# Folding w3 with w_out by plain f32 products, w_out converted in place, instead of by three products of high and low parts

## The chip, the cores and the metric

The kernel runs on one core of a Trainium2 chip. The metric is the device time of one execution in microseconds. TensorE is called PE, VectorE DVE, ScalarE ACT, GpSimd POOL, and SyncE, whose queue issues almost all loads, SP. What separates two versions from no change is about 0.3% (2.5 us).

## What is computed

Windowed attention (4 sequences of 576 tokens, 8 heads of 64) gives 2304 tokens of 512 values; two linear stages follow.

```python
x = attention(q, k, v)                     # 2304 x 512
a, b = x @ w1, x @ w2                      # 512 x 1024 each
y = (a * b) @ w3 @ w_out                   # w3 1024 x 1024, w_out 1024 x 512
h = y @ w_in                               # 512 x 2048
out = maximum(0.01 * h, h) @ w_out2        # 2048 x 512
```

The weights arrive as 64-bit words and are turned into f32 on the chip.

## The kernel before, in words

Since nothing nonlinear stands between w3 and w_out, the kernel first forms wf = w3 @ w_out ("the fold") and then uses (a*b) @ wf. Nearly all large products are made of three: each f32 operand is split into a high part, rounded to the type float32r, and the low part that is left, and `mm3` (L75 to L77) issues high x high, high x low and low x high.

A weight is converted in **units** of 512 KB (128 x 512 words). A unit is loaded (L280, four buffers `raw`), scaled on ACT (`f`, L299), its low bits fetched on ACT (`low`, L287, one buffer), shifted and merged on DVE (L316), given its sign on DVE (L311), and then finished. L311 is the last reader of the raw buffer: the load four units later waits for it. SP issues loads in one fixed order, with the loads of q, k and v for the first sequence between them: none behind the first six units, one behind each of the next ten, six behind each of the next eight.

Units 0 to 15 alternate between w3 (first half of its rows) and w_out, units 16 to 23 are the second half of w3, and from unit 24 on come w1 and w2. A w3 unit is finished by four transposes on PE (L353), the copy of the high part on ACT (L355) and the low part on DVE (L356). A w_out unit is finished by a cast on ACT (L260) and a subtraction on DVE (L261). Then the fold runs in sixteen **steps**, 0 to 7 for the first half of wf and 8 to 15 for the second. Step i multiplies the i-th transposed tile, which is unit 2i up to step 7 and unit i + 8 after it, with a tile of w_out, into four banks of 512 columns: 12 matmuls. After steps 7 and 15 the four banks are copied out as wf (L372 on ACT, L373 on DVE).

Attention of the first sequence is woven between the steps, twelve groups of scores (L176 on PE, plain f32), exponentials (L184), transposes (L203, copied by L205 to `pts`) and products with v (L230, copied by L236 to `x`). When the fold is done, the products x @ w1 and x @ w2 begin (tile `ab` at L75 to L77). A scheduler fixes each engine's order when the kernel is built, and each engine then runs its list strictly in that order.

Of the kernel before, what the change touches and what calls it, by code (L numbers as in the profile page):

```python
# [8 lines left out]
F32 = mybir.dt.float32  # L9
F32R = mybir.dt.float32r  # L10
# [4 lines left out]
ALU = mybir.AluOpType  # L15
# [6 lines left out]
def tile_kernel(ctx: ExitStack, tc: tile.TileContext, q, k, v, w1, w2, w3, w_out, w_in, w_out2, out):  # L22
# [18 lines left out]
    P = 128  # L41
# [4 lines left out]
    KF = DFF // P  # L46
# [10 lines left out]
    UC = 512  # L57
# [7 lines left out]
    act, dve, pool, pe, sp = nc.scalar, nc.vector, nc.gpsimd, nc.tensor, nc.sync  # L65

    def f32(ap):
        return ap.bitcast(F32)
# [5 lines left out]
    def mm3(ps, lh, ll, rh, rl, first, last, more=False):  # L74
        pe.matmul(ps, lhsT=lh, rhs=rh, start=first, stop=False, skip_group_check=more)  # L75
        pe.matmul(ps, lhsT=lh, rhs=rl, start=False, stop=False, skip_group_check=more)  # L76
        return pe.matmul(ps, lhsT=ll, rhs=rh, start=False, stop=last, skip_group_check=more).ins  # L77

    const = ctx.enter_context(tc.tile_pool(name="const", bufs=1))
    wpool = tc.alloc_tile_pool(name="wpool", bufs=1)  # L80
# [7 lines left out]
    stage = tc.alloc_tile_pool(name="stage", bufs=2, side="right")  # L88
# [6 lines left out]
    p0 = tc.alloc_tile_pool(name="p0", bufs=4, reuse_waits="tile")  # L95
# [144 lines left out]
    def wslot(key):  # L240
        pl, tag, bufs = wpool, "w", 8
        if key[0] == "wo2":
            pl, tag, bufs = (po1, "w1", 4) if key[1] < 4 else (po2, "w2", 4)
        elif key[0] == "wf":
            tag, bufs = "wf", 4
        return pl.tile([P, 2, 2 * UC], F32R, name=tag, tag=tag, bufs=bufs)

    def rows2(t):
        return t.rearrange("p s (l m) -> p s l m", l=2)
# [4 lines left out]
    def store(key, half):  # L254

        def fin(f):
            if key not in slots:
                slots[key] = wslot(key)
            t, sl = slots[key], slice(UC * half, UC * half + UC)
            act.copy(t[:, 0, sl], f)  # L260
            (pool if key[0] in ("w1", "w2") else dve).tensor_tensor(out=t[:, 1, sl], in0=f, in1=f32(t[:, 0, sl]),  # L261
                                                                     op=ALU.subtract)
        return fin

    units = []
    last = {}
    slots = {}
# [14 lines left out]
    def flat(t):  # L282
        return t.rearrange("p k m -> p (k m)") if len(t.shape) == 3 else t

    def low_bits(u):
        u["low"] = stage.tile([P, UC], I32, name="low", tag="low", bufs=1)
        act.activation(out=u["low"], in_=flat(u["raw"]).bitcast(U8).rearrange("p (m e) -> p m e", e=8)[:, :, 3],  # L287
                       func=AF.Copy, scale=1.0 / 32, bias=-31.0 / 64)

    def advance(stop):  # L290

        now = dict(n_of)
        if now["scale"] < min(stop, now["load"]):
            u = units[now["scale"]]
            w = flat(u["raw"]).bitcast(I32).rearrange("p (m two) -> p m two", two=2)
            u["lo"], u["hi"] = w[:, :, 0], w[:, :, 1]
            u["f"] = stage.tile([P, UC], F32, name="f", tag="f", bufs=4)
            with tc.issue_after(pss["copy"]) if now["scale"] >= PHASE_B else nullcontext():
                act.mul(u["f"], u["hi"].bitcast(F32), 2.0 ** -112)  # L299
                if now["scale"] < PHASE_B:  # L300
                    low_bits(u)
            n_of["scale"] += 1
        if now["fin"] < now["bits"]:
            u = units[now["fin"]]
            u["fin"](u["f"])
            n_of["fin"] += 1
        d = now["bits"] < now["shift"]
        if d:
            u = units[now["bits"]]
            f = u["f"].bitcast(I32)  # L310
            dve.scalar_tensor_tensor(out=f, in0=u["hi"], scalar=-0x80000000, in1=f, op0=ALU.bitwise_and, op1=ALU.bitwise_or)  # L311
        if now["shift"] < now["scale"]:
            u2 = units[now["shift"]]
            g = u2["f"].bitcast(I32)
            if "low" in u2:
                dve.scalar_tensor_tensor(out=g, in0=g, scalar=3, in1=u2["low"], op0=ALU.logical_shift_left, op1=ALU.bitwise_or)  # L316
            else:
                dve.tensor_scalar(g, g, 3, 0x7FFFFFF8, op0=ALU.logical_shift_left, op1=ALU.bitwise_and)
            n_of["shift"] += 1
        if d:  # L320
            if "low" not in u:
                dve.scalar_tensor_tensor(out=f, in0=u["lo"], scalar=29, in1=f, op0=ALU.logical_shift_right, op1=ALU.bitwise_or)
            n_of["bits"] += 1
            feed()

    def until(n, stop):
        while n_of["fin"] < n:
            advance(stop)

    def unit(src, fin, key):  # L330
        units.append({"src": src, "fin": fin})
        last[key] = len(units)
# [4 lines left out]
            unit(w[2 * P * h:2 * P * h + 2 * P, 2 * P * p:2 * P * p + 2 * P].rearrange("(k p) m -> p k m", p=P),  # L337
                 store((name, p), h), (name, p))

    def row_unit(w, name, l):  # L340

        unit(w[P * l:P * l + P, :], store((name, l // 2), l % 2), (name, l // 2))


    w3T = []
    wps = {}
    pss = {}

    def w3_tr(f):
        t = p0.tile([P, 2, 4, P], F32R, name="w3T", tag="w3T", bufs=2)  # L350
        ps = ps_ab.tile([P, 4, P], F32, name="ab", tag="ab")
        for i in range(4):
            pe.transpose(ps[:, i, :], f[:, P * i:P * i + P], ident)  # L353
        both = t.rearrange("p s i k -> p s (i k)")
        act.copy(both[:, 0], ps.rearrange("p i k -> p (i k)"))  # L355
        dve.tensor_tensor(out=both[:, 1], in0=ps.rearrange("p i k -> p (i k)"), in1=f32(both[:, 0]), op=ALU.subtract)  # L356
        w3T.append(t)

    def w3_mm(gi, l, half):
        t = w3T[0]  # L360
        wo = rows2(slots["wo", l // 2])
        for i in range(2 * half, 2 * half + 2):
            if l == 0:
                wps[i] = ps_mm.tile([P, DM], F32, name="mm", tag="mm")
            mm3(wps[i], t[:, 0, i, :], t[:, 1, i, :], wo[:, 0, l % 2], wo[:, 1, l % 2], l == 0, l == KF - 1)
        if half == 0:
            return
        w3T.pop(0)
        if l == KF - 1:
            for i in range(4):  # L370
                wf = rows2(slots["wf", 2 * gi + i // 2])
                act.copy(wf[:, 0, i % 2], wps[i])  # L372
                dve.tensor_tensor(out=wf[:, 1, i % 2], in0=wps[i], in1=f32(wf[:, 0, i % 2]), op=ALU.subtract)  # L373

    for gi in range(2):
        for l in range(KF):
            unit(w3[4 * P * gi:4 * P * gi + 4 * P, P * l:P * l + P].rearrange("(k p) m -> p k m", p=P), w3_tr, ("w3", gi, l))
            if gi == 0:
                row_unit(w_out, "wo", l)
    W12 = len(units)  # L380
    for p in range(KD):
        col_units(w1, "w1", p)
# [9 lines left out]
            unit(w_in[2 * P * h:2 * P * h + 2 * P, 2 * P * p:2 * P * p + 2 * P].rearrange("(k p) m -> p k m", p=P),  # L392
                 keep(2 * p + h), ("win", p, h))
    n_of["cap"] = KEPT = len(units)
    for name, p in [("wo", i) for i in range(4)] + [(n, p) for p in range(2) for n in ("w1", "w2")] + [("wf", i) for i in range(4)]:
        slots[name, p] = wslot((name, p))

    GPB = NHP * NG
# [4 lines left out]
    def plan_att(b, t0, span):  # L403

        order = [(hp, gr) for hp in range(NHP) for gr in range(NG)]
        if b == 0:
            order = order[:2 * NG] + [x for x in order[2 * NG:] if x[1] < 2] + [x for x in order[2 * NG:] if x[1] == 2]
        for j in range(GPB):
            t = clock["t"] + t0 + j * span // (GPB - 1)
            hp, gr = order[j]  # L410
            n = b * NHP + hp
            g = n * NG + gr
            pieces = [(-1, 2.5, prep_q, g), (0, 3, qk, g), (2, 0, rn, g)]
            pieces += [(LTR[1], 2, tp, g), (LAV[1], 1, av, g)] if b else [(LTR[0], 2, tr, g), (LAV[0], 1, av, g)]
            if gr == 0:
                pieces.append((-2, 2.4, prep_k, n))
            if gr == NG - 1 and n >= NHP - 1 and n + 1 < B * NHP:
                pieces.append((-1, 2.6, load_qk, n + 1))
            if gr == NG - 1 and (hp < 2 if b == 0 else n + 2 < B * NHP):
                pieces.append((LAV[b > 0], 1.5, load_v, n + (2 if b else NHP)))  # L420
            for d, r, f, n in pieces:
                ev.setdefault(max(t + d, clock["t"]), []).append((r, n, len(ev), f))
# [43 lines left out]
    for t in qbd_t:  # L466
        dve.memset(t, 0.0)
    its = [(gi, l) for gi in range(2) for l in range(KF)]
    until(last["wo", 0] - 1, W12)
    until(last["wo", 0] + 1, W12)  # L470
    plan_att(0, 6, 17)
    for i, (gi, l) in enumerate(its):
        w3_mm(gi, l, 0)
# [224 lines left out]
    for b in range(B):  # L698
        if b + 1 < B:
            plan_att(b + 1, *((10, 26) if b == 0 else (1, 37)))  # L700
        for s in range(2 * KF):
            hf, f = divmod(s, KF)
# [351 lines left out]
```

## Time and profile before

| | |
|---|---|
| time, median of 3 runs | 832.38 us (831.74 to 834.05) |
| span of the profiled execution, its own time here | 832.9 us |
| PE busy in the span | 796.3 us, 96% |
| DVE, ACT, POOL busy | 589.0, 447.9, 67.2 us |
| PE clock granted, mean | 0.993 |
| last matmul of the fold, start | about 104 us into the span |

The span is read from the first to the last instruction; the profile gives no time around it. A busy share is a mean over stages: the weight conversion and fold at the start, then the long matmul stages.

### The profile page before, as it was taken

The page shows a single profiled execution, that of the slowest core. Times are in us where ns is not written, and L with a number is a line of the kernel's source. Part 1 is how long each engine was busy: PE and PEld are TensorE (multiplying, and loading weights), DVE is VectorE, ACT ScalarE, POOL GpSimd, SP SyncE. Part 2 cuts the span into 40 slices and gives each one's busy share as a digit, 9 for nine tenths or more (in the row PEclk, how much of TensorE's full clock was granted, in tenths as well). Part 3 has the DMA queues.
Part 4 walks back from the last instruction along what each step waited for, and adds up shares of the span by engine and source line. Part 5 has one row for each costly group of instructions (what it writes and reads, how often), then busy time and mean ns, then how long its engine had stood idle before and what let it go on. Part 6 is the DMA issues. An engine that isn't in the chain of part 4 may idle for free.

```text
span 832.9 us, 16724 instructions
## 1 busy us (share of the span) xinstructions
PE 796.3 (96%) x5980; PEld 767.8 (92%) x5980; DVE 589.0 (71%) x1505; ACT 447.9 (54%) x1095; POOL 67.2 (8%) x77
## 2 busy tenths in 40 slices
PE   5778889999999999999999999999999999999998
PEld 3567679989999999999999999999999999999997
DVE  5798988653656438775751476877667999798976
ACT  6686985342434335443532455655556766665644
POOL 1012444110111101110000000000000000000000
PEclk9999989999999999999999999999999999999999
DMA  7799488665455526786530156998998754343331
GB/s 239 200 210 240 163 236 195 160 159 122 104 116 136 116 67 174 206 244 192 162 97 28 39 190 218 311 326 304 319 325 275 243 189 163 102 153 122 108 100 52
DMA packets 205507, 147.91 MB, mean 178 GB/s; under 512 B 136944, under 2 KB 171504, under 8 KB 205424
## 3 DMA queue, kind: packets, MB, share of 16 engines
q1 hardware_dynamic: 200672, 142.00, 58.5%
q10 hardware_dynamic: 4752, 4.85, 1.8%
q8 instruction: 47, 0.77, 0.4%
q14 instruction: 36, 0.29, 0.1%
HBM read 98.83 MB, written 47.97 MB: 176 GB/s over the span
## 4 chain that ended last, share of the span: by engine, by line
PE 79%; DMA 10%; DVE 4%; ACT 4%; issue 1%; SPq 1%; POOL 0%; DVEq 0%; ACTq 0%; POOLq 0%
PE o L76 7%; PE o L77 7%; PE o L75 7%; PE ab L75 7%; DMA raw<-in_moe_w_dram 7%; PE ab L77 7%; PE ab L76 7%; PE pr L75 7%; PE pr L77 7%; PE pr L76 7%; PE mm L75 4%; PE mm L76 4%; PE mm L77 4%; PE sc L176 3%; PE pa L230 2%; ACT f L299 1%
## 5 line engine op out<-in xcount | busy, mean ns | idle before, releaser
L75 PE MATMUL ab<-x,w 128*128 128x288 f32 x512 | 154.1, 301 | 3.9 <-ACT x L236 2.8
L77 PE MATMUL ab<-x,w 128*128 128x288 f32 x512 | 152.2, 297 | 0.0
L76 PE MATMUL ab<-x,w 128*128 128x288 f32 x512 | 152.2, 297 | 0.0
L75 PE MATMUL pr<-yop,w 128*128 128x384 f32 x300 | 101.3, 338 | 1.2 <-ACT c L654 1.2
L75 PEld LDWEIGHTS ab<-x,w 128*128 128x128 f32 x512 | 97.1, 190 | 5.5 <-ACT x L236 2.9
L77 PE MATMUL pr<-yop,w 128*128 128x384 f32 x300 | 101.0, 337 | 0.0
L76 PE MATMUL pr<-yop,w 128*128 128x384 f32 x300 | 100.8, 336 | 0.0
L76 PEld LDWEIGHTS ab<-x,w 128*128 128x128 f32 x512 | 97.3, 190 | 0.2
L77 PEld LDWEIGHTS ab<-x,w 128*128 128x128 f32 x512 | 97.2, 190 | 0.1
L654 ACT COPY c<-pr 128x384 f32<-128x384 f32 x95 | 45.3, 480 | 65.1 <-PE pr L77 58.7
L75 PE MATMUL mm<-ab,wf 128*128 128x288 f32 x256 | 76.4, 309 | 0.0
L77 PE MATMUL mm<-ab,wf 128*128 128x288 f32 x256 | 74.8, 294 | 0.0
L76 PE MATMUL mm<-ab,wf 128*128 128x288 f32 x256 | 74.6, 293 | 0.0
L76 PE MATMUL o<-yop,yop 128*128 128x256 f32 x259 | 73.0, 282 | 0.0
L77 PE MATMUL o<-yop,yop 128*128 128x256 f32 x259 | 72.9, 282 | 0.0
L75 PE MATMUL o<-yop,yop 128*128 128x256 f32 x259 | 72.9, 281 | 0.0
L503 DVE TENSOR_TENSOR p<-ab,a 128x288 f32<-128x288 f32 x64 | 28.8, 451 | 56.6 <-PE ab L77 56.2
L498 ACT COPY a<-ab 128x288 f32<-128x288 f32 x64 | 25.6, 399 | 79.5 <-PE ab L77 79.4
L184 ACT ACTIVATE s<-s,nm 128x128 f32<-128x128 f32 x144 | 56.6, 396 | 19.1 <-DVE nm L180 18.2
L193 POOL TENSOR_TENSOR s<-s,rs 128x384 f32<-128x384 f32 x48 | 41.3, 860 | 293.1 <-DVE rs L192 209.3
L657 DVE TENSOR_TENSOR c<-pr,c 128x384 f32<-128x384 f32 x74 | 40.8, 554 | 29.8 <-PE pr L77 17.6
L791 ACT CAST yop<-raw 128x256 fp32r<-128x256 f32 (+1 forms) x92 | 42.5, 485 | 35.6 <-PE o L76 34.8
(129 smaller groups left out, 2083.1 us busy)
## 6 DMA issues: line engine op xcount, KB each, us to landing
hd<-c SPq DMA_DIRECT2D x96, 192.0 KB, 3.7
raw<-in_moe_w_dram SPq DMA_DIRECT2D x32, 512.0 KB, 4.5
raw<-hd SPq DMA_DIRECT2D x32, 512.0 KB, 3.7
raw<-in_moe_w_out_dram SPq DMA_DIRECT2D x24, 512.0 KB, 4.7
raw<-in_moe_w_in_dram SPq DMA_DIRECT2D x16, 512.0 KB, 4.8
wd<-f SPq DMA_DIRECT2D x32, 256.0 KB, 3.7
raw<-wd SPq DMA_DIRECT2D x30, 256.0 KB, 4.8
vt<-in_v_dram SPq DMA_DIRECT2D x56, 128.0 KB, 2.8
```

The source lines that it names most:

```text
L75: pe.matmul(ps, lhsT=lh, rhs=rh, start=first, stop=False, skip_group_check=more)
L76: pe.matmul(ps, lhsT=lh, rhs=rl, start=False, stop=False, skip_group_check=more)
L77: return pe.matmul(ps, lhsT=ll, rhs=rh, start=False, stop=last, skip_group_check=more).ins
L176: pe.matmul(sc[:, t, :], lhsT=qb[:, t, :], rhs=kT[n][:, k0:k0 + P], start=True, stop=True)
L184: act.activation(out=s[:, t, :], in_=s[:, t, :], func=AF.Exp, bias=nm[:, t:t + 1], scale=-1.0, accum_out=sm[:, t:t + 1])
L193: pool.tensor_tensor(out=s, in0=s, in1=rs.unsqueeze(2).to_broadcast([P, GT, P]), op=ALU.mult)
L230: pe.matmul(o[W * h:W * h + W, W * t:W * t + W], lhsT=vt[:, a, h, m, :], rhs=pts[:, 2 * h:2 * h + 2, t], start=True, stop=True)
L498: pss["copy"] = act.copy(pss["a"], ps).ins
L503: dve.tensor_tensor(out=p32, in0=ps, in1=pss["a"], op=ALU.mult)
L654: pss["copy"] = act.copy(self.sb[to], ps).ins
L657: pss["add"] = dve.tensor_tensor(out=self.sb[to], in0=self.ps[at], in1=self.sb[of or to], op=ALU.add).ins
L791: tied("act", lambda: act.copy(out, x))
```

## The change

The fold multiplies f32 tiles directly. The transposed w3 tile is copied once, as f32, into one of four buffers (before: two parts, two buffers). The w_out units are no longer split: their conversion writes into two tiles `wo_home` that stay, and finishing them does nothing.

```diff
-            u["f"] = stage.tile([P, UC], F32, name="f", tag="f", bufs=4)
+            u["f"] = u["home"]() if "home" in u else stage.tile([P, UC], F32, name="f", tag="f", bufs=4)
...
-        unit(w[P * l:P * l + P, :], store((name, l // 2), l % 2), (name, l // 2))
+        unit(w[P * l:P * l + P, :], lambda f: None, ("wo", l))
+        units[-1]["home"] = lambda: wo_home[l // 4][:, l % 4]
...
-        t = p0.tile([P, 2, 4, P], F32R, name="w3T", tag="w3T", bufs=2)
+        t = p0.tile([P, 4, P], F32, name="w3T", tag="w3T", bufs=4)
...
-        both = t.rearrange("p s i k -> p s (i k)")
-        act.copy(both[:, 0], ps.rearrange("p i k -> p (i k)"))
-        dve.tensor_tensor(out=both[:, 1], in0=ps.rearrange("p i k -> p (i k)"), in1=f32(both[:, 0]), op=ALU.subtract)
+        act.copy(t, ps)
...
-            mm3(wps[i], t[:, 0, i, :], t[:, 1, i, :], wo[:, 0, l % 2], wo[:, 1, l % 2], l == 0, l == KF - 1)
+            pe.matmul(wps[i], lhsT=t[:, i, :], rhs=wo, start=l == 0, stop=l == KF - 1)
...
+    wo_home = [wpool.tile([P, 4, UC], F32, name="wo", tag="w", bufs=8) for _ in range(2)]
```

The scheduler orders the engines anew. On DVE, at the very start of the conversions, the list before reads as follows (L356 and L261 are the low parts of w3 and w_out):

```order
L316 SCALAR_TENSOR_TENSOR f<-f,low 128x512
L356 TENSOR_TENSOR w3T<-ab,w3T 128x512
L311 SCALAR_TENSOR_TENSOR f<-raw,f 128x512
L261 TENSOR_TENSOR w<-f,w 128x512
L316 SCALAR_TENSOR_TENSOR f<-f,low 128x512
```

and now, at the same place:

```order
L316 SCALAR_TENSOR_TENSOR f<-f,low 128x512
L311 SCALAR_TENSOR_TENSOR f<-raw,f 128x512
L316 SCALAR_TENSOR_TENSOR wo<-wo,low 128x512
L311 SCALAR_TENSOR_TENSOR wo<-raw,wo 128x512
L316 SCALAR_TENSOR_TENSOR f<-f,low 128x512
```

L311, which frees a raw buffer, now has no operation before it that waits for PE or for a cast on ACT.

On ACT, around the copy that step 8 needs, the list before is this; the first `f` is unit 18, the L355 under it the copy of step 8, the last `f` unit 19:

```order
L299 ACTIVATE f<-raw 128x512
L205 COPY pts<-ab 128x3x4x32
L355 CAST w3T<-ab 128x512
L287 ACTIVATE low<-raw 128x512
L372 CAST wf<-mm 128x512
...
L372 CAST wf<-mm 128x512 x2
L236 CAST x<-pa 128x192
L205 COPY pts<-ab 128x3x4x32
L299 ACTIVATE f<-raw 128x512
```

and now, where the first `f` is unit 18, the second unit 19, and the copy of step 8 is the last row:

```order
L299 ACTIVATE f<-raw 128x512
L287 ACTIVATE low<-raw 128x512
L371 CAST wf<-mm 128x512 x4
L236 CAST x<-pa 128x192
L299 ACTIVATE f<-raw 128x512
L287 ACTIVATE low<-raw 128x512
L205 COPY pts<-ab 128x3x4x32
L355 COPY w3T<-ab 128x512
```

The copy of step 8 has moved behind unit 19. On PE, between step 7 (first row) and step 8 (last row), the new list is

```order
L364 MATMUL mm<-wo,w3T 128x512 x4
L176 MATMUL sc<-kT,qbd_95 128x128 x3
L230 MATMUL pa<-pts,vt 64x64 x6
L203 MATMUL ab<-ident,s 128x128 x3
L354 MATMUL ab<-ident,f 128x128 x4
L176 MATMUL sc<-kT,qbd_93 128x128 x3
L364 MATMUL mm<-wo,w3T 128x512 x4
```

With the rows ahead of it, step 8 has four score groups, two transposes of probabilities and one product with v before it; before the change it had six, four and two. So two, two and one of them now stand behind its start.

## Rows read from the trace of the kernel before

**Rows 1.** Stretches: length, busy PE, PEld, DVE, ACT, POOL, granted clock, DMA share, GB/s.

```profile
8.00:41.67 33.67, 24.94 (x98) 18.39 (x97) 25.40 (x49) 22.50 (x41) 0.00 (x0) 0.95 0.78 211
41.67:81.00 39.33, 33.00 (x236) 26.81 (x235) 35.75 (x123) 29.10 (x92) 7.62 (x9) 1.00 0.96 219
61.77:104.22 42.45, 37.37 (x268) 29.70 (x267) 36.81 (x109) 33.72 (x95) 14.25 (x13) 1.00 0.72 201
...
108.86:115.00 6.14, 6.13 (x30) 5.29 (x31) 5.50 (x11) 4.89 (x10) 2.70 (x3) 0.50 0.85 194
...
118.00:833.00 715.00, 707.43 (x5430) 697.10 (x5428) 492.22 (x1258) 360.45 (x884) 40.15 (x42) 1.00 0.58 171
```

**Rows 2.** PE's groups, 0 to 104.3 us: count, busy, mean ns, idle before.

```profile
L75 PE MATMUL mm<-w,w3T 128*128 128x512 f32 x64 | 24.6, 450 | 12.4 <-ACT w L260 7.6 <-ACT w3T L355 4.7
...
L176 PE MATMUL sc<-kT,qbd 128*128 128x128 f32 x72 | 10.4, 280 | 0.0
```

**Rows 3.** PE in order of time: start, duration, operation, count, idle before.

```profile
37.09 0.40 PE L76 MATMUL mm<-w,w3T 128*128 128x512 f32 x1
...
38.24 0.40 PE L77 MATMUL mm<-w,w3T 128*128 128x512 f32 x1
...
57.78 0.57 PE L230 MATMUL pa<-pts,vt 128*64 128x64 f32 x12
58.28 0.55 PE L203 MATMUL ab<-ident,s 128*128 128x128 f32 x3
58.67 0.83 PE L176 MATMUL sc<-kT,qbd 128*128 128x128 f32 x6
59.34 0.60 PE L353 MATMUL ab<-ident,f 128*128 128x128 f32 x4
...
61.77 0.48 PE L75 MATMUL mm<-w,w3T 128*128 128x512 f32 x1
```

**Rows 4.** DVE's groups, 0 to 104 us.

```profile
L356 DVE TENSOR_TENSOR w3T<-ab,w3T 128x512 fp32r<-128x512 f32 x16 | 10.9, 679 | 2.1 <-ACT w3T L355 2.1
...
L261 DVE TENSOR_TENSOR w<-f,w 128x512 fp32r<-128x512 f32 x8 | 5.8, 727 | 0.7 <-ACT w L260 0.7
```

**Rows 5.** ACT's groups, same stretch; six of these casts are of w1 and w2.

```profile
L260 ACT CAST w<-f 128x512 fp32r<-128x512 f32 x14 | 8.7, 619 | 0.4 <-DVE f L311 0.3
```

**Rows 6.** What SP's queue waited for, 0 to 110 us: total, times, longest.

```profile
SPq L280 <- DVE f L311: 50.7, 21, 4.9
```

**Rows 7.** Chain that ended last, in order of time: start, length, what.

```profile
33.84 2.08 PE mm L75 x4
...
36.81 0.60 ACT w3T L355
...
41.67 4.38 DMA raw<-in_moe_w_dram
```

**Rows 8.** SP in order of time: issue start, duration; units 4, 16 and 19.

```profile
7.29 0.38 SPq L280 DMA_DIRECT2D raw<-in_moe_w_dram  x1
...
41.67 0.38 SPq L280 DMA_DIRECT2D raw<-in_moe_w_dram  x1
...
56.03 0.43 SPq L280 DMA_DIRECT2D raw<-in_moe_w_dram  x1
```

**Rows 9.** DMA issues by line, whole span: KB each, us to landing.

```profile
raw<-in_moe_w_dram SPq DMA_DIRECT2D x32, 512.0 KB, 4.5
```

**Rows 10.** ACT in order of time, for unit 23.

```profile
80.75 0.69 ACT L299 ACTIVATE f<-raw 128x512 f32<-128x512 f32 x1 [1.33 <-DMA raw<-in_moe_w_dram]
...
82.36 0.31 ACT L236 CAST x<-pa 128x192 fp32r<-128x192 f32 x1
```

**Rows 11.** ACT in order of time, behind the end of the fold.

```profile
106.52 1.54 ACT L372 CAST wf<-mm 128x512 fp32r<-128x512 f32 x3
...
108.46 0.34 ACT L236 CAST x<-pa 128x192 fp32r<-128x192 f32 x1
```

**Rows 12.** PE in order of time, its first wait behind the fold.

```profile
108.86 0.99 PE L75 MATMUL ab<-x,w 128*128 128x288 f32 x2 [2.79 <-ACT x L236]
```

More of the change, by code (lines that the diff above doesn't have):

```diff
@@ L338, in col_units, with row_unit @@
                  store((name, p), h), (name, p))
-    def row_unit(w, name, l):
-        unit(w[P * l:P * l + P, :], store((name, l // 2), l % 2), (name, l // 2))
+    def row_unit(w, l):
+        unit(w[P * l:P * l + P, :], lambda f: None, ("wo", l))
+        units[-1]["home"] = lambda: wo_home[l // 4][:, l % 4]
     w3T = []
@@ L360, in w3_mm @@
         t = w3T[0]
-        wo = rows2(slots["wo", l // 2])
+        wo = wo_home[l // 4][:, l % 4]
         for i in range(2 * half, 2 * half + 2):
@@ L378, in tile_kernel @@
             if gi == 0:
-                row_unit(w_out, "wo", l)
+                row_unit(w_out, l)
     W12 = len(units)
@@ L394, in tile_kernel @@
     n_of["cap"] = KEPT = len(units)
-    for name, p in [("wo", i) for i in range(4)] + [(n, p) for p in range(2) for n in ("w1", "w2")] + [("wf", i) for i in range(4)]:
+    wo_home = [wpool.tile([P, 4, UC], F32, name="wo", tag="w", bufs=8) for _ in range(2)]
+    for name, p in [(n, p) for p in range(2) for n in ("w1", "w2")] + [("wf", i) for i in range(4)]:
         slots[name, p] = wslot((name, p))
@@ L468, in tile_kernel @@
     its = [(gi, l) for gi in range(2) for l in range(KF)]
-    until(last["wo", 0] - 1, W12)
     until(last["wo", 0] + 1, W12)
+    until(last["wo", 1] + 1, W12)
     plan_att(0, 6, 17)
```

## The prediction

> **What bounds the kernel now.** I read first the busy time by stretch, to find where TensorE is not already full. From 118 us to the end PE is busy 707.4 of 715.0 us [rows 1]; nothing in that part changes in its work. So the change can only move the moment at which PE gets there, and what counts is when the fold ends (its last matmul starts near 104 us) and how the wait behind it goes. In the fold PE has room: from 8.00 to 41.67 us it is busy 24.94 of 33.67 us [rows 1].
>
> Next I read what PE waited for and what paced it. In the groups of PE, the high-part matmuls L75 had 12.4 us of idle time before them, 7.6 for the cast of a w_out tile and 4.7 for the copy of a w3 tile [rows 2]. Those are the nearest releasers; the chain shows what stands behind them: PE at 33.84, the w3 copy on ACT at 36.81, and through DVE to a load that is issued only at 41.67 [rows 7]. SP's queue waited 50.7 us in 21 waits for the sign operation L311 [rows 6], the one that frees a raw buffer. So up to step 7 the fold runs at the pace of the loads, and these at the pace at which buffers come free. From 41.67 to 81 us the DMA engines are busy 0.96 of the time against 0.78 before [rows 1]: there the loads themselves are the limit. From step 8 (61.77 us) to 104.22 PE is busy 37.37 of 42.45 us [rows 1]: there PE is nearly the bound, and work added to it shows.
>
> **The change, part by part.**
>
> *PE's products.* Six split matmuls start 0.23 us apart (37.09 to 38.24 us, five intervals) [rows 3], so the 12 of a step cost 2.76 us. What a plain f32 matmul with 512 columns costs, no row shows. The nearest are the scores: plain f32, 128 columns, recorded as two instructions for each matmul (72 in the stretch for 36 matmuls [rows 2]). Six of them take from 58.67 to 59.34, 0.112 us each [rows 3]. If the time goes with the columns, an instruction of 512 columns takes at most 4 x 0.112 = 0.447 us. From below, it cannot be less than the 0.23 of a split matmul of as many columns. I take 0.44, near the scores, since they are the same kind of operation. A step is then 8 x 0.44 = 3.52 us, 0.76 more than now: 12.2 us over sixteen steps, 6.1 of them in steps 8 to 15.
>
> The Trainium skill ("FP8 and Floating Point Precision", section TensorE Precision Notes) says that a true f32 matmul makes four passes through the array. That speaks against the lower end: by an estimate from it, four passes of 512 columns at 2.4 GHz are 0.853 us per product, and 5.2 us instead of 6.1 for the eight steps. No row here shows it for 512 columns.
>
> *DVE and ACT.* Gone are 16 subtractions of 679 ns and 8 of 727 ns on DVE, 16.7 us [rows 4], and 8 casts of 619 ns on ACT, 5.0 us [rows 5]. By themselves they are worth nothing: what counts is that they stood before L311, waiting for PE or ACT, and delayed the loads.
>
> *The loads.* Units 4 to 16 are issued in 34.4 us, from 7.29 to 41.67 [rows 8], 2.87 us each. How much faster they get no row shows. At most the DMA engines get as full as later: 33.67 us x 0.78 / 0.96 = 27.4 us, a gain of 6.3. At least the gap that ends at 41.67 closes in part: the copy at 36.81 [rows 7] no longer waits for a matmul held up by the w_out cast, an estimate of 2 out of the 3.0 us between PE's late start at 33.84 and that copy. Below nothing it can't go, since the loads keep their order. I take 4 us, the middle. From unit 16 on SP issues six attention loads behind each unit at a DMA share of 0.96, and that lead is only kept.
>
> *The moved copy.* Step 8's w3 copy now stands behind unit 19 on ACT, not unit 18. Unit 19's load is issued at 56.03 [rows 8] and lands 4.5 us later [rows 9], at 60.5; 4 us earlier is 56.5. From the scaling of a unit to the end of the copy behind it ACT takes 82.36 - 80.75 = 1.6 us for unit 23 [rows 10], and here a probability copy is between them, about 0.5: step 8 can start at 58.6, 3.2 us before the 61.77 of now [rows 3]. The lead of the loads is thus mostly kept, but PE sits idle between steps 7 and 8, since the work there is short.
>
> *What stands behind that start.* Today 37.4 us of PE work [rows 1]. Added: 6.1 for the dearer products, and the groups that the new order has put behind step 8: two of scores at 0.67, two of transposes at 0.39, one of products with v at 0.50 [rows 3], 2.6 us. Today 5.1 us of that stretch are idle; I take 4, since longer matmuls cover more of the waits for ACT's copies. The end of the fold: 58.6 + 37.4 + 6.1 + 2.6 + 4 = 108.7, 4.5 us later than 104.2.
>
> *Behind the fold.* PE waits 2.79 us for a copy of x [rows 12], which on ACT stands behind the copies of wf (106.52 to 108.46) [rows 11]. More of w1 and w2 is then converted, and one load's landing less may hold ACT: I take 1 us back. Then 832.9 + 4.5 - 1 = 836.4 for the profiled execution; the median of the runs shown is 0.5 below that execution, so 836, which is 0.4% slower.
>
> DVE and the memory of the tiles cost nothing further: wo's two tiles take places in the pool that the four split ones had, and the fourfold buffer of w3 tiles takes as much as the twofold one had.
>
> **The rivals.**
>
> *The loads fill the DMA engines and the idle time is absorbed.* For it: PE's matmuls are longer, and DVE's list no longer waits for PE at all at the start. Step 8 starts 2.3 us earlier than above, at 56.3, and half of the idle goes: 56.3 + 37.4 + 6.1 + 2.6 + 2.5 = 104.9. With 1 us back the time is 832.6 for the execution, 832 for the median: no change. Against it: ACT's list still holds each w3 copy behind a later unit's landing.
>
> *Faster: the clock does not drop behind the fold.* After the 2.79 us wait the granted clock is 0.50, the lower level of 1.2 GHz, from 108.86 to 115.00 [rows 1, 12]; 6.1 us there do the work of 3. If the x copy comes early enough for the wait to stay clearly below 2.79 us, those 3 us are saved and 1 more of the wait. On top of the full load gain that gives 828, on top of my own sum 832. It decides from the point where ACT is through its wf copies about 1 us sooner after the fold than now. Against it: the ACT list still has these copies and conversions before the x copy.
>
> *One pass only.* If a plain instruction of 512 columns takes 0.23 us, a step costs 1.84: 7.4 us less over steps 8 to 15 instead of 6.1 more. The fold then ends at 108.7 - 13.5 = 95.2 and the kernel near 823. Against it: a quarter of 0.23 is 0.057, and the scores take 0.112 us for a quarter of the columns.
>
> *The loads gain nothing.* If the DMA engines give no more with more loads under way, the lead of 4 us is gone: 840. The share of 0.78 against 0.96 speaks against it.
>
> **How the numbers follow.** My forecast, 836, has a chance of 0.47, and its own range is 833.5 to 838.5 (loads 2 to 6.3 us, price 0.427 to 0.447, idle 3 to 5). The full loads without change: 0.22. The clock held: 0.13. One pass: 0.05. Loads without gain: 0.13. 0.3% of the median, about what a measurement of this kernel can tell from no change, is 2.5 us: below 829.9 is faster, above 834.9 slower. Faster gets one pass and most of the held clock with full loads, 0.15. No change gets the second case, the rest of the third and a part of the forecast's lower side, 0.32. Slower gets 0.53. The range 829 to 841 leaves out one pass and a part of the third case below and a little above.
>
> **What the profile after would show.** The plain products, two records each, 0.43 to 0.45 us apart at full clock, 128 of them; if 0.23, the price was wrong. SP's wait for L311 well below 50.7 us and unit 16 issued near 37.7; the DMA share from 8 to 38 us near 0.9. Step 8 starting near 58.6 with a wait for the w3 copy before it. PE busy over 45 us from there to the end of the fold, near 108.7. Behind it one wait for x of 2 to 3 us. From there to the end the same 715 us of work. What would make me wrong: an order of ACT that turns out harmless because the loads come much earlier than I think, or a wait of over 2.79 us between steps 7 and 8 that lowers the clock there.

## The result, and the profile after

The changed kernel takes 838.61 us, the median of 8 runs (834.29 to 840.8). The kernel before took 833.19 us in the same session (8 runs, 829.65 to 835.46). The ratio is 1.0067, with a 95% interval of 1.0045 to 1.009: slower by 0.45 to 0.9%. The profiled execution took 839.88 us, with a span of 838.1 us against 832.9 before.

The page of the changed kernel, its span and the busy time of its engines:

```profile
span 838.1 us, 16567 instructions
...
PE 807.3 (96%) x5916; PEld 755.8 (90%) x5916; DVE 582.5 (70%) x1481; ACT 444.9 (53%) x1087; POOL 66.6 (8%) x77
```

PE is busy 11.0 us more than before and the span is 5.2 us longer. Where those are is read from the stretches. First two of before that were not shown yet, the start of the conversions and the stretch from the fold's end to the first product with wf (columns as in [rows 1]):

```profile
8.00:38.00 30.00, 21.27 (x81) 15.81 (x80) 21.79 (x36) 19.17 (x34) 0.00 (x0) 0.94 0.82 219
104.22:119.15 14.93, 12.13 (x92) 10.76 (x90) 13.08 (x27) 11.79 (x26) 6.92 (x5) 0.77 0.93 245
119.15:832.90 713.75, 706.28 (x5421) 695.95 (x5419) 491.07 (x1256) 359.30 (x881) 40.15 (x42) 1.00 0.58 171
```

The changed kernel, cut at its own step 8, fold end and first product with wf:

```profile
8.00:38.00 30.00, 28.32 (x86) 14.03 (x85) 22.20 (x37) 20.21 (x36) 0.00 (x0) 1.00 1.05 262
...
44.80:50.00 5.20, 5.20 (x8) 2.19 (x9) 2.52 (x12) 1.74 (x8) 0.82 (x1) 0.67 0.77 163
56.53:61.65 5.12, 5.12 (x9) 2.08 (x9) 3.99 (x16) 3.61 (x14) 1.14 (x2) 0.70 0.89 194
56.53:108.23 51.70, 47.57 (x267) 28.14 (x267) 37.46 (x122) 39.37 (x116) 17.14 (x16) 0.97 0.65 180
108.23:124.00 15.77, 11.09 (x92) 9.87 (x90) 15.61 (x30) 12.36 (x29) 6.78 (x5) 0.89 0.73 182
118.00:121.00 3.00, 2.96 (x12) 2.97 (x13) 2.91 (x8) 2.21 (x4) 1.02 (x1) 0.50 0.52 167
124.00:838.00 714.00, 706.77 (x5420) 696.06 (x5418) 492.05 (x1250) 357.59 (x876) 38.46 (x42) 1.00 0.58 171
```

From the first product with wf on, both kernels take the same time (713.75 and 714.0 us). So nearly all of the loss is there when that product starts: 124.00 against 119.15, 4.85 us. The start of the conversions is fuller than before: PE 28.32 of 30 us instead of 21.27, the DMA share 1.05 instead of 0.82. Yet step 8 begins at 56.53, 5.2 us earlier than before [rows 3], the fold ends at 108.23, 4.0 us later, and behind the fold 0.8 us more is lost. (108.23 is the start of the last step below, 104.79, plus the 3.44 us of a step.) Steps 7 and 8, which start at 44.80 and 56.53, run at a granted clock of 0.67 and 0.70 in the mean, where the stretch of before from step 8 on had 1.00 [rows 1].

PE in order of time (start, duration, operation, count, idle before):

```profile
21.57 3.60 PE L364 MATMUL mm<-wo,w3T 128*128 128x512 f32 x8
25.01 0.60 PE L354 MATMUL ab<-ident,f 128*128 128x128 f32 x4
...
43.28 0.55 PE L203 MATMUL ab<-ident,s 128*128 128x128 f32 x3 [1.28 <-POOL s L193]
44.80 5.40 PE L364 MATMUL mm<-wo,w3T 128*128 128x512 f32 x8 [0.97 <-ACT w3T L355]
...
51.67 0.60 PE L354 MATMUL ab<-ident,f 128*128 128x128 f32 x4
54.30 0.94 PE L176 MATMUL sc<-kT,qbd 128*128 128x128 f32 x6 [2.02 <-DVE nm L180]
56.53 5.19 PE L364 MATMUL mm<-wo,w3T 128*128 128x512 f32 x8 [1.30 <-ACT w3T L355]
...
104.79 3.60 PE L364 MATMUL mm<-wo,w3T 128*128 128x512 f32 x8
...
112.29 0.78 PE L75 MATMUL ab<-x,w 128*128 128x288 f32 x2 [2.20 <-ACT x L236]
...
118.04 0.61 PE L75 MATMUL ab<-x,w 128*128 128x288 f32 x1 [1.98 <-ACT a L498]
...
124.00 0.70 PE L75 MATMUL mm<-ab,wf 128*128 128x288 f32 x4
```

The first two rows are the price: eight plain records, four products, start at 21.57 and the next operation at 25.01, so 3.44 us a step and 0.43 a record. The group's mean duration must not be taken for that, since the records overlap:

```profile
L364 PE MATMUL mm<-wo,w3T 128*128 128x512 f32 x128 | 64.6, 648 | 4.0 <-ACT w3T L355 4.0
```

What held step 8 stands in the chain that ended last, between 43 and 60 us:

```profile
43.57 6.26 DMA raw<-in_moe_w_dram
50.20 4.18 DMA raw<-in_moe_w_dram
54.40 0.68 ACT f L299
55.08 0.56 ACT low L287
55.63 0.36 ACT pts L205
55.99 0.49 ACT w3T L355
56.53 3.47 PE mm L364 x4
```

This is ACT's order as the change made it: unit 19 lands, is scaled, its low bits and one probability copy follow, and only then comes the copy for step 8. And this is SP's queue, with the loads of units 16 and 19:

```profile
31.60 0.38 SPq L280 DMA_DIRECT2D raw<-in_moe_w_dram  x1
33.11 5.83 SPq L461 DMA_DIRECT2D x<-in_q_dram  x4
...
50.20 0.43 SPq L280 DMA_DIRECT2D raw<-in_moe_w_dram  x1
```

Unit 16 is issued 10.1 us earlier than before, unit 19 only 5.8 [rows 8]. Between them four small loads of q, of 72 KB each, hold SP for 5.83 us; before, the same four took it 3.15.

### The profile page after: what moved, and what is told of

The parts are those of the page before. It is cut to its first block, busy times and chain, and to the rows that moved or that the text cites. A ratio compares the mean times of both kernels' runs of the same rounds, so it can differ in the third digit from the quotient of the medians.

```text
span 838.1 us, 16567 instructions
## 1 busy us (share of the span) xinstructions
PE 807.3 (96%) x5916; PEld 755.8 (90%) x5916; DVE 582.5 (70%) x1481; ACT 444.9 (53%) x1087; POOL 66.6 (8%) x77
## 3 DMA queue, kind: packets, MB, share of 16 engines
q10 hardware_dynamic: 4752, 4.85, 1.7%
## 4 chain that ended last, share of the span: by engine, by line
PE 82%; DMA 10%; DVE 4%; ACT 3%; issue 1%; SPq 0%; POOL 0%; DVEq 0%; ACTq 0%
PE ab L75 7%; PE o L76 7%; PE o L77 7%; PE o L75 7%; PE ab L76 7%; PE ab L77 7%; PE pr L75 7%; PE pr L77 7%; PE pr L76 7%; DMA raw<-in_moe_w_dram 5%; PE mm L75 4%; PE mm L77 3%; PE mm L76 3%; PE sc L176 3%; PE pa L230 3%; PE mm L364 2%
## 5 line engine op out<-in xcount | busy, mean ns | idle before, releaser
L364 PE MATMUL mm<-wo,w3T 128*128 128x512 f32 x128 | 64.6, 648 | 4.0 <-ACT w3T L355 4.0
L504 ACT CAST ab<-p 128x288 fp32r<-128x288 f32 x64 | 27.7, 433 | 65.6 <-DVE p L503 65.6
```

Source lines behind the costliest of these rows:

```text
L364: pe.matmul(wps[i], lhsT=t[:, i, :], rhs=wo, start=l == 0, stop=l == KF - 1)
L504: act.copy(t[:, 0], p32)
```

## The experiments

Three theories were put to the test. **A:** the plain products cost time because PE is nearly full, and the removed split work gives some of it back. **B:** the new order on ACT, the copy of step 8 behind unit 19, is what costs. **C:** the removed work on DVE and ACT gives nothing. The code shown is cut at "...". In what follows "over before" is the median of a kernel less that of the kernel before in the same session (832.88, 832.49 and 832.87 us); the change itself stands at +5.4 us. The ratio's interval is in brackets.

### The two parts of the change apart

The change without its price: three bf16 products of 512 columns take the place of each plain one, 0.225 us apart.

```diff
...
-            pe.matmul(wps[i], lhsT=t[:, i, :], rhs=wo, start=l == 0, stop=l == KF - 1)
+            th, wh = (x.bitcast(BF16).rearrange("p (m two) -> p m two", two=2)[:, :, 1] for x in (t[:, i, :], wo))
+            mm3(wps[i], th, th, wh, wh, l == 0, l == KF - 1)
```

> The changed kernel with the fold's products at the old price: three 16-bit matmuls per product on the upper halves of the words, with no low parts (so that part of the fold's precision is left out). Work removed from DVE and ACT as in the change, PE work about as before. Theory A (the price of the plain products on PE is what costs): 8 to 12 us of PE work less than the changed kernel, of which the part in steps 8 to 15 shows, so 829 to 833 us, no slower than before. Theory B (the new order of ACT, which holds each w3 copy behind later units, is what costs): the order stays nearly the same, so 836 to 839. Theory C (the removed DVE and ACT work gives nothing): 833.

The price without the change: the kernel before keeps its splits and multiplies only the high parts, by plain f32 products.

```diff
-            mm3(wps[i], t[:, 0, i, :], t[:, 1, i, :], wo[:, 0, l % 2], wo[:, 1, l % 2], l == 0, l == KF - 1)
+            pe.matmul(wps[i], lhsT=f32(t[:, 0, i, :]), rhs=f32(wo[:, 0, l % 2]), start=l == 0, stop=l == KF - 1)
```

> The kernel before with plain f32 products on the high parts only (the low parts are still computed, but left out of the products): the old DVE and ACT work, the new price on PE. Theory A: the loads get no lead and the price of 0.68 us a step is paid in full in steps 8 to 15 and in part before, so 839 to 844 us, slower than the changed kernel by what its loads gain. Theory B: the ACT list is that of before, so 833 to 835. Theory C: the same as the changed kernel, 838 to 839.

| | split work kept | split work gone |
|---|---|---|
| three cheap products | before, 0 | 824.58 us, -8.3 [0.9876, 0.9917] |
| plain f32 products | 840.8 us, +7.9 [1.0069, 1.0108] | the change, +5.4 [1.0045, 1.009] |

The first time, 824.58, is below every range expected for it; the second lies in that of A. The price costs 7.9 us with the splits kept and 13.7 with them gone. Taking the split work out gives 8.3 us where the products are cheap; where they are dear it is 2.5, and there the two intervals overlap, so that it is not shown to be more than nothing. The two cheap products are not quite alike: the split ones start 0.23 us apart, the bf16 ones 0.225, which is about 1 us over the 192 of the fold, so up to that much of the 8.3 may be theirs. A holds: the removal is a real gain where the products are cheap, and the dearer products take it and more. C falls there and is open at the plain price. The two do not simply add: the price is dearer by 5.8 us without the split work.

### The order on ACT

The w3 copy moved to DVE, away from ACT's list:

```diff
-        act.copy(t, ps)
+        dve.tensor_copy(out=t, in_=ps)
```

> The changed kernel with the copy of the transposed w3 tile on DVE instead of ACT, so that no copy stands behind the scaling of a later unit on ACT. Theory A: PE's price stays; of the waits for the copies (some 8 us of PE idle time in all) 2 to 4 us come back: 834 to 837. Theory B: the whole loss comes back and the half-speed stretches go: 830 to 833. A third possibility: the copies now wait behind DVE's conversions and attention, no gain: 838 to 841.

843.82 us, +10.9 [1.0104, 1.0144]. The wait of PE for the copy grows instead of going away; its group of products:

```profile
L364 PE MATMUL mm<-wo,w3T 128*128 128x512 f32 x128 | 66.5, 671 | 6.7 <-DVE w3T L355 6.7
```

The time is above even the range of the third possibility. DVE has the shifts and signs of the units in its list, and the copy waits behind those. So this run does not speak against B; it shows only that DVE is the worse place.

The order itself, put back: a unit is finished before the next is scaled (the added lines are moved up from behind the scaling), and the scaling of every unit from 16 on is listed after the last w3 copy.

```diff
...
+        if now["fin"] < now["bits"]:
+            u = units[now["fin"]]
+            u["fin"](u["f"])
+            n_of["fin"] += 1
...
-            with tc.issue_after(pss["copy"]) if now["scale"] >= PHASE_B else nullcontext():
+            with (tc.issue_after(pss["copy"]) if now["scale"] >= PHASE_B else
+                  tc.issue_after(pss["w3c"]) if 2 * KF <= now["scale"] else nullcontext()):
...
-        act.copy(t, ps)
+        pss["w3c"] = act.copy(t, ps).ins
```

> The changed kernel with ACT's order forced: from unit 16 on, a unit is scaled only behind the w3 copy of the unit three before it, so that the copy of step 8 stands ahead of unit 19's scaling. If the moved copy costs (my step 'the moved copy'), step 8 starts 2 to 4 us before its 56.5 and the time is 834 to 837. If PE's price alone is the cause, the start is earlier but the work behind it waits later instead: 838 to 840.

838.4 us, +5.9 [1.0045, 1.0079]: nothing gained. But the place changed. The last matmuls of the fold now start at 98.88 instead of 104.79, and the time is lost behind them. From 80 to 104 us, first the change, then this kernel:

```profile
80.00:104.00 24.00, 20.76 (x122) 11.79 (x120) 19.07 (x52) 20.10 (x57) 11.75 (x10) 1.00 0.40 121
```

```profile
80.00:104.00 24.00, 22.52 (x135) 12.47 (x133) 8.07 (x30) 13.79 (x41) 3.36 (x5) 1.00 0.20 65
```

The edit also holds back the units of w1 and w2. DVE is busy for 8.07 us where it was for 19.07. Behind the fold PE then waits 2.2 us for w1 and w2 (1.4 for their casts on ACT, 0.8 for POOL), where the change has no such wait, and from 98.88 to 126 us its granted clock is 0.87. That spoils the run as a test of B, so it was made again with the rule for units 16 to 23 alone:

```diff
-                  tc.issue_after(pss["w3c"]) if 2 * KF <= now["scale"] else nullcontext()):
+                  tc.issue_after(pss["w3c"]) if 2 * KF <= now["scale"] < W12 else nullcontext()):
```

> As e5_copy_before_unit, but the forced order holds back only units 16 to 23, no longer the units of w1 and w2, whose conversions in e5 all moved behind the last w3 copy and were late for the products after the fold. If the moved copy costs: the fold ends 3 to 6 us before the 108.2 of the changed kernel and that reaches the end, 833 to 836. If the price alone counts: 838 to 840.

836.3 us, +3.4 [1.0017, 1.0052], 2.0 us better than the change. The two intervals overlap a little, so this is at the edge of what can be told, and the time is just above the range for a copy that costs. Step 8 begins at 54.34 instead of 56.53, and it is the attention work ahead of it that now waits, and behind the wait runs at a granted 0.50 (51.31 to 54.34 us):

```profile
51.31 0.91 PE L230 MATMUL pa<-pts,vt 128*64 128x64 f32 x12 [2.30 <-ACT pts L205]
...
54.34 5.21 PE L365 MATMUL mm<-wo,w3T 128*128 128x512 f32 x8
```

The copy now stands ahead of unit 19 again, as in the kernel before, and 3.4 of the 5.4 us stay. So B holds for a part of the loss at most, and this run alone hardly shows that part.

### The price, half by half

The three bf16 products in steps 0 to 7 alone:

```diff
...
+            if gi == 0:
+                mm3(wps[i], th, th, wh, wh, l == 0, l == KF - 1)
+            else:
+                pe.matmul(wps[i], lhsT=t[:, i, :], rhs=wo, start=l == 0, stop=l == KF - 1)
```

> The changed kernel with the old price (three 16-bit products on the upper halves, low parts left out) in steps 0 to 7 and plain products in steps 8 to 15. My prediction counted the price in steps 8 to 15 alone: then this is 836 to 839, as the changed kernel. If the price is paid in every step alike: 831 to 833, half way to e1_no_split_cheap (824.6).

and in steps 8 to 15 alone (`if gi == 1`):

> The changed kernel with plain products in steps 0 to 7 and the old price in steps 8 to 15 (three 16-bit products, low parts left out). If the price counts in steps 8 to 15 alone: 824 to 828, near e1_no_split_cheap. If it is paid in every step alike: 831 to 833.

828.82 us, -4.1 [0.993, 0.9965], for the first half, and 827.79, -5.1 [0.9909, 0.996], for the second. With the change and the kernel without the price this is a table of four, in us over before:

| | steps 8 to 15 cheap | steps 8 to 15 plain |
|---|---|---|
| steps 0 to 7 cheap | -8.3 | -4.1 |
| steps 0 to 7 plain | -5.1 | +5.4, the change |

The price of steps 0 to 7 is 3.2 us where the other half is cheap and 9.5 where it is plain; that of steps 8 to 15 is 4.2 and 10.5. They cost more together than apart. Each half's cost is clear of the noise except for the 3.2, where the intervals of the two kernels just overlap ([0.9876, 0.9917] and [0.9909, 0.996]). Of the expectations, 828.82 is below both ranges, and 827.79 lies in the one for a price that counts in steps 8 to 15 alone; the 9.5 us of the first kernel speak against that.

How each half does so shows in the stretch from step 8's start to the first product with w1. In the change:

```profile
56.53:107.83 51.30, 47.17 (x267) 27.98 (x267) 37.18 (x121) 38.97 (x116) 17.14 (x16) 0.97 0.65 179
```

with steps 0 to 7 cheap:

```profile
50.32:100.55 50.23, 46.49 (x266) 27.73 (x267) 38.65 (x118) 40.98 (x116) 18.48 (x17) 0.97 0.80 210
```

and with steps 8 to 15 cheap:

```profile
54.09:96.61 42.52, 40.95 (x322) 25.81 (x323) 33.23 (x121) 36.77 (x114) 13.91 (x14) 0.98 0.67 184
```

With the second half cheap, PE's work behind step 8 shrinks by 6.2 us (47.17 to 40.95) and the idle time there from 4.1 to 1.6. That profile is of the shortest of its runs, 2.8 us below their median, so its idle time may be on the low side. With the first half cheap, the work behind step 8 is the same to 0.7 us, and step 8 just starts 6.2 us earlier. The loads do not explain this: unit 18 is issued at 45.62 there, 2.0 later than in the change, and unit 19 at 50.58, 0.4 later. PE's list shows where the 6.2 us are. In the kernel with the first half cheap, these are the starts of step 7, of the transposes for step 8, and of step 8:

```profile
43.26 0.40 PE L76 MATMUL mm<-wo,w3T 128*128 128x512 bf16 x1 [1.59 <-ACT w3T L356]
...
47.96 0.60 PE L355 MATMUL ab<-ident,f 128*128 128x128 f32 x4
...
50.32 1.99 PE L369 MATMUL mm<-wo,w3T 128*128 128x512 f32 x4 [1.50 <-ACT w3T L356]
```

In the change they are 44.80, 51.67 and 56.53. So 1.5 us are there when step 7 starts, 2.2 come up to the transposes, and 2.5 up to step 8. The last part is ACT's list. The copy of step 8, and unit 18 behind it:

```profile
49.67 0.60 ACT L356 COPY w3T<-ab 128x512 f32<-128x512 f32 x1
...
51.14 0.69 ACT L300 ACTIVATE f<-raw 128x512 f32<-128x512 f32 x1
```

The first part is ACT's list too: the copy of step 7 stands behind unit 17 in the change (44.18 and 43.06) and ahead of it here (42.65 and 45.11). The middle part is step 7 itself, 0.74 us by the price (3.44 us for 2.70) and most of the rest by the clock: a granted 0.67 over step 7 in the change, 1.00 here. These are single profiles: the kernel with steps 8 to 15 cheap has the same products in steps 0 to 7 as the change, but it runs step 7 at full clock in 3.53 us and starts step 8 at 54.09, 2.4 us before the change.

The scheduler lists the work anew for every edit, and the place of step 8's copy goes with the products of steps 0 to 7. Where these are plain (the change, the dear split kernel, this pair's second kernel, the mixed kernel below) it stands behind unit 19; where they are cheap, behind unit 18 (before) or ahead of it (both kernels with bf16 products there). So what I had listed as two edits, a price and a moved copy, is in the first half partly one: the dearer products move the copy. Whether the scheduler goes by their time or by their number (4 for 12 in a step) was not tested. What the better list alone is worth is not shown: the order put back by hand, which got the copy ahead of unit 19 only, gave 2.0 us, and of the 6.2 us here some 4 are in the list, in one profile. A list with the copy ahead of unit 18 at the full price was not run.

### Looking for a version that beats both

If the price hurts most where PE is full, plain products belong in steps 0 to 7 and split ones in steps 8 to 15. w_out is then kept in f32 and split from there by POOL (a copy and a subtraction), and the w3 tiles are split only from step 8 on:

```diff
...
+            if gi == 0:
+                pe.matmul(wps[i], lhsT=f32(t[:, 0, i, :]), rhs=wo, start=l == 0, stop=l == KF - 1)
+            else:
+                ws = rows2(slots["wo", l // 2])
+                mm3(wps[i], t[:, 0, i, :], t[:, 1, i, :], ws[:, 0, l % 2], ws[:, 1, l % 2], l == 0, l == KF - 1)
```

> Plain products in steps 0 to 7, where PE waits for loads, and three split products in steps 8 to 15; w_out is split by GpSimd from its f32 tile. Theory A: the lead of the loads is kept and 5 to 6 us of PE price in the second half are gone: 830 to 833 us, about as fast as before or a little faster. Theory B: the ACT order costs as in the changed kernel: 836 to 839.

833.07 us, +0.2 [0.9977, 1.0009]: as before. (The kernel sets aside two places fewer for w1 and w2 at the start; their fifth cast still begins at 99.19, where it was 101.41 before, so that is not seen to hold it back.) The first product with w1 starts at 101.98, about 2.2 us earlier than before, and the next wait, 2.79 us long before [rows 12], is now 4.06:

```profile
107.88 0.78 PE L75 MATMUL ab<-x,w 128*128 128x288 f32 x2 [4.06 <-ACT x L236]
```

So the same kernel once more with the second half's wf copies listed behind the tenth copy of x on ACT (`xc[9]`), and the kernel before with that edit alone:

```diff
...
-                act.copy(wf[:, 0, i % 2], wps[i])
+                with tc.issue_after(xc[9]) if gi else nullcontext():
+                    act.copy(wf[:, 0, i % 2], wps[i])
```

> The kernel with plain products in steps 0 to 7 only, and the copies of the second half of wf put behind the copy of x on ACT. In the run without this, PE waited 4.1 us for that x copy and ran at half speed behind it. If the wf copies are what holds it: 828 to 831. If ACT is held by a unit whose load has not landed: 832 to 834.

> The kernel before with the copies of the second half of wf behind the same copy of x. Before, PE waited 2.8 us there and then ran at half speed for 6.1 us. If the wf copies are what holds the x copy and the clock stays up: 827 to 830. If not: 832 to 834.

834.54 us, +2.1 [1.0013, 1.0039], and 833.44, +1.0 [0.9988, 1.0019]: no gain in either, and the first is even half a microsecond above its range. In the kernel before the wait does fall, from 2.79 to 1.52 us, and the clock stays whole behind it (1.00 from 104 to 126 us):

```profile
103.89 0.78 PE L75 MATMUL ab<-x,w 128*128 128x288 f32 x2 [1.52 <-ACT x L237]
```

But the time does not. In that one profile the first product with wf starts at 112.97, 6.2 us before that of [rows 12]'s kernel, and the span is only 3.2 shorter: work is done in another order, and part of it comes back behind the mark. The median says no gain at all.

Two more versions join the mixed kernel with the order on ACT: with the wide rule and the wf copies, then with the rule for units 16 to 23 alone. Their edits are those above.

> The kernel with plain products in steps 0 to 7 only, with that forced order on ACT and with the copies of the second half of wf behind the copy of x for which PE waits after the fold. If both waits cost: 826 to 830, faster than before. If they are only moved: 832 to 834.

> Plain products in steps 0 to 7 only, with the forced order of ACT for units 16 to 23. If the wait of step 8 for unit 19 costs there too: 828 to 831, faster than before. If it is given back behind the fold: 832 to 835.

838.22 us, +5.7 [1.004, 1.0073], above both of its ranges: a wait of 4.85 us for a product on DVE behind the fold, and a clock of 0.989 over the whole span. And 834.17, +1.3 [0.9997, 1.0028]. No version with all of the products beat the kernel before. Those that do (the cheap ones) leave the low parts out and are no candidates.

## Why the prediction was right, and where a step was not

The forecast was 836.0 us, from 829 to 841; the time is 838.61. The sign and most of the mechanism hold; one step on the price fell, three sizes were off, and that the sum came out so near is in part luck, since errors cancel.

**The price** was taken as 0.44 us from the scores; it is 0.43. A product is two records, 0.86 us. The rival of a single pass falls. The Trainium skill ("FP8 and Floating Point Precision", TensorE Precision Notes) counts four passes for true f32, which gave an estimate of 0.853 us; the trace, with 0.86, agrees in the time, and shows two records, not four.

**Where the price shows: the step that fell.** I counted it in steps 8 to 15 alone, 6.1 us of work, and that term was right, 6.2 us by the kernel with those steps cheap. In steps 0 to 7 I took it as absorbed in PE's idle time, because the loads set the pace there. As work it is: PE goes to 28.32 of 30 us, and unit 16 comes no later. But it costs there too: 9.5 us with steps 8 to 15 plain as in the change, 3.2 with them cheap, which the noise hardly tells from nothing. One way is ACT's list, in which the changed kernel has the copies of steps 7 and 8 each behind one more unit than before; another is step 7 itself, which runs at a granted 0.67 behind waits of 1.28 and 0.97 us. How the 9.5 us divide between the two is open. I had the list in the sum, as the moved copy of step 8, without seeing that it came from the price; so the sum held where its parts were told wrongly.

**The loads.** I gave a lead of 4 us at unit 16, with a bound of 6.3 at a DMA share of 0.96. It was 10.1, since the share reached 1.05. But I said that the lead would then be kept, and it was not: 7.9 us were left at unit 18 and 5.8 at unit 19. SP's wait for the sign operations hardly fell, from 50.7 us in 21 waits [rows 6] to 43.6 in 17 and 5.2 in 6:

```profile
SPq L280 <- DVE f L311: 43.6, 17, 7.3
SPq L280 <- DVE wo L311: 5.2, 6, 1.2
```

I had expected well below 50.7. The wait is only moved: up to 42 us it fell from 28.8 to 17.6, and from there to 110 us it rose from 21.9 to 31.2. From 7 to 38 us the loads of 512 KB took 6.0 us to land, where they took 4.4 and 5.0 before.

**The moved copy.** Step 8 was to start at 58.6, held by unit 19; the chain shows just that, at 56.53. The 2.1 us are those by which the load came sooner than I took.

**Behind that start** I summed 50.1 us and it is 51.7. The idle time is the 4 I took (51.70 - 47.57 = 4.1). What I lacked is the clock: step 8 begins after waits of 2.02 and 1.30 us, and runs its 5.12 us at a granted 0.70; a step's eight records take 5.19 us instead of 3.60. That is the 1.6 us. I had named it as something that would make me wrong only above a wait of 2.79 us. The fold's end, 108.23 for a forecast 108.7, comes out right because this error and that of the start cancel, which is luck.

**Behind the fold: the size furthest off.** I took 1 us back and 0.8 us was lost (15.77 against 14.93). The wait for x did get shorter, 2.20 us for 2.79, and the clock held there. But then come a wait of 1.98 us for ACT's copy of a and half the clock, 0.50, from 118 to 121 us. The span adds up: fold end 0.5 better than forecast, this stretch 1.9 worse, 0.3 behind it, so +5.2 instead of +3.5. (The prediction's last 0.5 us set a span, 832.9, against a median of times; in the runs here a time is about 1.8 us longer than its span. The forecast does not change by this: it is 832.38 + 3.5 either way.)

The rival in which the clock is held lost on that same stretch: its condition, a shorter wait for x, came true, and another wait dropped the clock. The rival in which the loads gain nothing falls with unit 16, and the one in which the idle time is absorbed falls with the 4.1 us that stayed, though its first half came true: with the DMA engines full it had step 8 start at 56.3.

## What to carry to other kernels

Weigh dearer products by where the engine is full: here the removed split work was worth 8.3 us as long as the products stayed cheap, and the price took 13.7. Where the engine is idle a price can still cost, because the scheduler, with other products to place, lists other engines' work differently; so read in the new lists which load stands ahead of each copy that gates a step. And a gain at the head of a chain of loads is worth only what is left of it at the load that gates: of 10.1 us at unit 16, 5.8 were left at unit 19.

## What the hardware showed unexpectedly

With loads issued sooner the DMA engines went to a share of 1.05 and 262 GB/s from 8 to 38 us, where 0.96 had looked like the limit [rows 1]; and right there four small loads of q took SP 5.83 us to issue, for 3.15 before.

The clock fell after waits shorter than I expected. In the kernel before it stood at 0.50 behind a wait of 2.79 us. In the changed one it was 0.67 in the mean over step 7, behind waits of 1.28 and 0.97 us, and 0.50 from 118 us on behind a wait of 1.98, after 2.20 and 0.50 just before it, while right behind the 2.20 alone PE ran on at full rate. In the other direction, a wait of 1.52 us after the fold, with 1.14 and 0.53 soon after it, left it whole in the kernel before with the wf copies moved. So the length of the last wait alone did not tell here whether the clock would fall.
